# The first two triangular inverses of a delta-rule and mixture-of-experts kernel, done as 16-row triangles with TensorE corners

## The chip, the cores and the metric

The program runs on one core of a Trainium2 chip. The metric is the device time of one execution in microseconds, from the first to the last instruction and a little around it; lower is better.

## What is computed

A delta-rule attention with 4 batches, 8 heads, 768 positions and head size 48 feeds a mixture of four experts, and that feeds a gated layer:

```python
for t in range(S):
    y[:, :, t] = einsum('bhd,bhde->bhe', q[:, :, t], state)
    v_old = einsum('bhde,bhd->bhe', state, kt)
    state = state + bt * einsum('bhd,bhe->bhde', kt, vt - v_old)   # kt: normalized key
...
out += p[:, e:e + 1] * (np.maximum(x @ w1[e], 0.0) @ w2[e])         # 3072 x 384, hidden 1024, 4 experts
...
return (sigmoid(x @ w_gate) * (x @ w_val)) @ w_out                  # hidden 1536
```

## The kernel before

The 768 positions are cut into 12 steps of 64 (`C`). Within a step the recurrence is solved at once: with L the strictly triangular matrix of key products (the Gram) times the weights `w_all`, one needs the inverse of the unit triangle I + L for each of 32 (batch, head) pairs. All big products are done with operands split into a high and a low part, three matmuls for one. The attention of steps 2 to 11 is woven into the expert phases by a planner: `plan(...)` gives tasks a due time, and they are put into the stream of weight products as these pass that time. Only steps 0 and 1 come ahead of everything, in `startup()`, written out by hand in program order; the change lies in that function, in its helpers, and in the first two planned tasks.

What `startup()` does, engine by engine, each in the order of the program:

- **TensorE (PE)**: a warm-up; key Grams of steps 0 and 1 (L408, `pg`) and query products (`pq`); Grams of step 3 from `dec_a` and `dec_b` (L396); 60 padding products of zeros (`PADS`, L1297); Grams of step 2 from `KQ`, of step 4 from two `ws` tiles, of step 5 again from `dec_a` and `dec_b`; then step 0's chain: `pu` three times (inverse, corner, inverse), `py`, the transposes `pt` (L765); then the expert units `ph` (L910), with the state products `ps` (L745) of step 0 and the chain of step 1 (`pk`, `pu`) between them.
- **VectorE (DVE)**: norms, L (`LP`), masked query products (`YQ`), and then the inverse: steps 0 and 1 side by side, two 32-row triangles for each pair of a batch and a head in 128 partitions, by substitution. Substitution row s multiplies the finished columns by row s of L (`itmp`) and subtracts (`Xpp`). `invert(t0, t1)` does a piece of rows, transposes it (`x_cross`, into `ACC`) and has it copied into `XT` (`x_place`).
- **ScalarE (ACT)**: copies the Grams out of PSUM, into `LP` for steps 2 and 3 (L443), and for steps 4 and 5 (`grams_out`, L1274) into spare tiles, from which **GpSimd (POOL)** stores them in DRAM (`raw_d`) for later.
- **SP's DMA queue**: L goes out to DRAM (`ls`) and comes back in the inverse's layout (`Lpp<-ls`, by `l_read`). `both` deals the pieces of `l_out` and `l_read` out to SP's and ACT's queue by turns. `landed(t)` is a tiny DMA that waits until `t` has landed, so that what stands behind it on SP isn't issued earlier: `KQ` and the two `ws` loads (step 4's keys) stand behind the landing of `dec_b`, the next `dec_a` and `dec_b` (step 5's keys) and the first weights behind that of `KQ`.

The 32-row triangles leave the corner of the 64-row triangle out; it is put in by products with `Ld` (L's off-diagonal block) between two products with the inverse. Tiles that matter below: `XT` and `XT1`, the inverses of steps 0 and 1; `Lpp` and `Xpp`, flat scratch (`Lflat`, `Xflat`); `R`, right-hand sides; `U` in `Y`, intermediate; `rhsA`, `rhsB`, solved sides; `k2` in `Lflat`, keys for the norms of steps 2 and 3; `at`, two PSUM banks that `bank()` deals out.

Of the kernel before, what the change touches and what calls it, by code (L numbers as in the profile page):

```python
# [41 lines left out]
PADS = 60  # L42
# [74 lines left out]
def moe_delta_kernel(  # L117
# [50 lines left out]

    ident_sb = cp.tile([P, P], F32, name="ident_sb")
    mask_sb = cp.tile([P, C], F32, name="mask_sb")  # L170
# [473 lines left out]
    XC = ACC[:, 0:2].rearrange("p k c -> p (k c)").rearrange("p (t m) -> p t m", m=HC)  # L644
    Lc1 = ACC[:, 2].rearrange("p (g t) -> p g t", t=HC)
    XT1 = [gp.tile([P, 2 * STEP], F32, tag=tag, name="XT1").rearrange("p (h b t) -> p h b t", h=4, b=2) for tag in ("gv", "sg")]

    def x_cross(t0, t1):
        vec.transpose(out=XC[:, t0:t1], in_=x_view(0)[:, :, t0:t1].rearrange("p j t -> p t j"))

    def x_place(copy, c, g, t0, t1):
        i, a = divmod(g, 2)
        at, cols = slice(g * HC, (g + 1) * HC), slice(a * HC + t0, a * HC + t1)
        for k, t in enumerate(XT1 if c else [XT]):
            n = t.shape[1]
            src = XC[at, t0:t1].rearrange("p t (h c b) -> p t h c b", h=H, c=2)[:, :, k * n : (k + 1) * n, c]
            copy(out=t[at, :, :, cols], in_=src.rearrange("p t h b -> p h b t"))
# [511 lines left out]
    def startup():  # L1169
# [24 lines left out]
        l_init(0)  # L1194
        for t in (XT, Ld, *XT1, rhsA[C:112], rhsB[0:C], KI[C:112, 0], KI[0:C, 1], YQ[C:112, 0], YQ[0:C, 1]):
            nc.gpsimd.memset(t, 0.0)
# [10 lines left out]
        norm_move(0, 2)  # L1207
        q[1] = None
# [27 lines left out]
        load_ki(0)  # L1236
        spare = [((ph_p, "ph"), (acc_p, "acc1")), ((acc_p, "acc2"), (at_p, "at"))]
# [23 lines left out]
        store = [(gp, "gv"), (gp, "sg")] + [(hp, "hhi"), (hp, "hlo")] * 3  # L1261
        seats = {(4, 0): ((ph_p, "ph"), (acc_p, "acc1")), (4, 1): ((ph_p, "ph"), (acc_p, "acc2"))}
        seats |= {(5, 0): ((acc_p, "acc0"), (acc_p, "acc1")), (5, 1): ((acc_p, "acc2"), (ph_p, "ph"))}
# [13 lines left out]
        ops, cuts = [fn for _, fn in inv_ops(0, 2)], []  # L1277
        for n in range(HC - 1):
            cuts.append((cuts[-1] if cuts else 0) + 2 * min(2, n + 1))

        def invert(t0, t1, last=0):
            for fn in ops[(cuts[t0 - 2] if t0 else 0) : cuts[t1 - 2]]:
                fn()
            x_cross(t0, t1)
            for g in range(4):
                x_place(vec.tensor_copy if g < last else nc.scalar.copy, 0, g, t0, t1)
# [25 lines left out]
        invert(16, 24)  # L1312
        for hg in range(2):
            grams_mm(5, hg, KQ5)
        grams_out(5, 0)
        invert(24, 28)
        invert(28, 32, 2)
        norm_load(k2, 2)
        load_p(0)
        load_p(1)  # L1320
# [8 lines left out]
        grams_out(5, 1)  # L1329
        for g in range(4):  # L1330
            x_place(nc.gpsimd.tensor_copy, 1, g, 0, HC)
        sub = w_cast()
        for hs in sets:
            for b, pu in enumerate(quads("pu", ld, hs)):
                vec.tensor_tensor(out=R[:, b, hs], in0=R[:, b, hs], in1=pu[:, hs], op=ALU.subtract)
        pus = [quads("pu", x_of(0), hs) for hs in sets]
        for i in range(2):
            for hs, pu in zip(sets, pus):
                for rhs, at in ((rhsA, HALVES[0]), (rhsB, HALVES[1])):
                    if i and hs.start:  # L1340
                        for h in range(hs.start, hs.stop):
                            nc.scalar.activation(out=rhs[at, i, h], in_=pu[i][at, h], func=AF.Copy, scale=w_all[at, i, h : h + 1])
                        continue
                    wv = w_all[at, i, hs].unsqueeze(2).to_broadcast([C, hs.stop - hs.start, D])
                    vec.tensor_tensor(out=rhs[at, i, hs], in0=pu[i][at, hs], in1=wv, op=ALU.mult)
        q[0] = sp
        free[:] = free[:2]
        sub()
        for i in range(2):
            y_task(0, i)  # L1350
        scale_v(1)
# [34 lines left out]
        back["inv"] += first  # L1386

    with tc.manual_schedule():
        pre_lo = xp.tile([P, KT, 2 * STEP], F32R, tag="xlo", name="pre_lo")
        dec_tiles()  # L1390
        startup()
# [120 lines left out]
```

## Time and profile before

| | |
|---|---|
| median of 3 runs | 1401.55 us (1400.56 to 1403.18) |
| the profiled execution, its own time | 1401.91 us |
| span of the profiled execution | 1400.2 us |
| PE busy | 1367.8 us, 98% of the span |
| DVE, ACT, POOL busy | 1023.8, 568.9, 184.5 us |
| DMA | 237.09 MB, mean 169 GB/s |

A busy share is an average over the whole span. TensorE's granted clock is written as a share of full speed: 1.00 is 2.4 GHz and 0.50 is 1.2 GHz. The trace lists two rows for one fp32 product of the small kind (64 rows in the trace for 32 instructions in the program). A bracket at the end of a timeline's row gives the idle time of the engine just before it and what ended it.

### The profile page before, as it was taken

The numbers are of one execution on the slowest core, as the hardware profiler recorded it, in microseconds if no ns is written. First come the engines' busy times: TensorE is split into PE (matmuls) and PEld (weight loads), VectorE is DVE, ScalarE is ACT, GpSimd is POOL, SyncE is SP. The second block draws the span as 40 slices with busy tenths as digits, with TensorE's granted clock in tenths as the row PEclk, the third lists the DMA queues.
The fourth block names the chain that finished last, engine by engine and source line by source line (L and its number), as shares of the span: only waits on it lengthen the run. The fifth ranks groups of instructions, "written<-read, shape, count | busy, mean of one in ns | idle before, by whom it ended". The sixth has DMA issues, their size and how long they took to land.

```text
span 1400.2 us, 25468 instructions
## 1 busy us (share of the span) xinstructions
PE 1367.8 (98%) x10039; PEld 1131.7 (81%) x10039; DVE 1023.8 (73%) x1814; ACT 568.9 (41%) x943; POOL 184.5 (13%) x252
## 2 busy tenths in 40 slices
PE   6789999999999999999999999999999999999998
PEld 6678878878888888888888888888888888888887
DVE  6779988859998687887677887677787745444543
ACT  3665555443333343422444433344333334333333
POOL 3421222210112100011200011210000110000000
PEclk7799999999999999999999999999999999999999
DMA  9768997765556864565864465775435563434431
GB/s 244 240 208 253 322 307 226 221 176 173 160 149 157 199 174 143 145 191 137 204 185 136 152 182 143 181 194 139 132 107 133 151 177 102 132 109 121 109 107 57
DMA packets 105184, 237.09 MB, mean 169 GB/s; under 512 B 30360, under 2 KB 34648, under 8 KB 103512
## 3 DMA queue, kind: packets, MB, share of 16 engines
q1 hardware_dynamic: 86376, 189.95, 44.2%
q0 software_dynamic: 15504, 44.35, 14.0%
q8 instruction: 79, 1.29, 0.4%
q10 hardware_dynamic: 3184, 1.16, 0.4%
q14 instruction: 41, 0.34, 0.1%
HBM read 195.15 MB, written 26.79 MB: 159 GB/s over the span
## 4 chain that ended last, share of the span: by engine, by line
PE 84%; DVE 8%; DMA 4%; ACT 2%; issue 2%; ACTq 0%; SPq 0%; DVEq 0%
PE ph L910 43%; PE acc L947 35%; PE pu L630 1%; DMA raw<-in_wp 1%; DVE Xpp L144 1%; PE yt L699 1%; DVE ws L144 1%; DVE itmp L144 1%; DMA raw<-w_d 1%; PE pg L396 1%; PE ps L745 1%; DVE hlo L144 1%; PE pk L630 1%; ACT ws L231 1%; DMA Lpp<-in_wp 0%
## 5 line engine op out<-in xcount | busy, mean ns | idle before, releaser
L910 PE MATMUL ph<-xhi,ws 128*128 128x512 f32 (+1 forms) x2064 | 626.7, 387 | 1.4 <-ACT xhi L767 1.1
L947 PE MATMUL acc<-hhi,ws 128*128 128x512 f32 (+1 forms) x1632 | 493.7, 384 | 2.6 <-ACT dec_a L276 1.6
L910 PEld LDWEIGHTS ph<-xhi,ws 128*128 128x128 f32 x2064 | 381.1, 188 | 79.7 <-ACT xhi L767 1.6
L910 PE MATMUL ph<-xlo,ws 128*128 128x512 f32 (+1 forms) x1032 | 394.8, 385 | 1.5 <-DVE xlo L144 1.4
L947 PEld LDWEIGHTS acc<-hhi,ws 128*128 128x128 f32 x1632 | 302.1, 188 | 65.2 <-ACT YQ L275 2.0
L144 DVE TENSOR_TENSOR ws<-raw,ws 128x768 fp32r<-128x768 f32 x308 | 292.9, 956 | 51.4 <-ACT ws L231 47.8
L947 PE MATMUL acc<-hlo,ws 128*128 128x512 f32 (+1 forms) x816 | 312.5, 383 | 0.5 <-DVE hlo L144 0.5
L917 ACT ACTIVATE hhi<-ph 128x512 fp32r<-128x512 f32 (+1 forms) x200 | 116.1, 581 | 463.2 <-PE ph L910 463.2
L231 ACT CAST ws<-raw 128x768 fp32r<-128x768 f32 x308 | 252.6, 830 | 37.1 <-DMA raw<-w_d 21.9
L144 DVE SCALAR_TENSOR_TENSOR hlo<-ph,hhi 128x512 fp32r<-128x512 f32 (+1 forms) x200 | 133.4, 667 | 144.5 <-ACT hhi L917 144.4
L910 PEld LDWEIGHTS ph<-xlo,ws 128*128 128x128 f32 x1032 | 193.5, 188 | 42.4 <-DVE xlo L144 3.9
L947 PEld LDWEIGHTS acc<-hlo,ws 128*128 128x128 f32 x816 | 153.3, 188 | 31.0 <-DVE hlo L144 0.8
L144 DVE TENSOR_TENSOR itmp<-Xpp,Lpp 128x62 f32<-128x62 f32 (+29 forms) x344 | 158.1, 467 | 11.2 <-DMA Lpp<-ls 5.3
L144 DVE TENSOR_TENSOR Xpp<-Xpp,itmp 128x62 f32<-128x62 f32 (+29 forms) x344 | 156.7, 463 | 5.3
L926 ACT CAST hhi<-gv 128x512 fp32r<-128x512 f32 x72 | 44.7, 621 | 160.0 <-DVE gv L144 160.0
L144 DVE TENSOR_TENSOR gv<-ph,sg 128x512 f32<-128x512 f32 x72 | 49.7, 690 | 77.0 <-PE ph L910 73.7
L144 DVE TENSOR_TENSOR hlo<-gv,hhi 128x512 fp32r<-128x512 f32 x72 | 50.9, 707 | 49.4 <-ACT hhi L926 49.4
L989 POOL DMA_DIRECT2D ACC<-ctmp x39 | 34.6, 1177 | 366.4 <-DVE ctmp L144 366.4
L924 ACT ACTIVATE sg<-ph 128x512 f32<-128x512 f32 x72 | 42.8, 594 | 47.2 <-PE ph L910 47.2
L474 POOL DMA_DIRECT2D ld<-LP x12 | 8.1, 678 | 315.5 <-DVE LP L144 315.5
L144 DVE TENSOR_TENSOR ctmp<-acc,pe 128x512 f32<-128x512 f32 (+1 forms) x57 | 35.4, 656 | 8.6 <-PE acc L947 7.8
L630 PEld LDWEIGHTS pu<-R,XT 64*64 64x64 f32 x1024 | 18.3, 140 | 12.6 <-issue 9.3
(189 smaller groups left out, 837.6 us busy)
## 6 DMA issues: line engine op xcount, KB each, us to landing
raw<-in_wp SPq DMA_DIRECT2D x200, 384.0 KB, 3.2
raw<-w_d SPq DMA_DIRECT2D x108, 384.0 KB, 3.8
ACC<-ctmp POOLq DMA_DIRECT2D x33, 256.0 KB, 5.4
KQ<-in_kg SPq DMA_DIRECT2D x7, 896.0 KB, 7.9
Lpp<-ld POOLq DMA_DIRECT2D x8, 768.0 KB, 11.0
pe<-p_d SPq DMA_DIRECT2D x23, 256.0 KB, 5.9
dec_a<-in_wp SPq DMA_DIRECT2D x15, 384.0 KB, 5.7
Lpp<-in_wp SPq DMA_DIRECT2D x14, 384.0 KB, 5.6
```

What stands on the lines that cost most here:

```text
L144: return fn(*args, **kw)
L231: nc.scalar.copy(out=w[:, 0], in_=t)
L396: nc.tensor.matmul(out=pg[i][b * C : (b + 1) * C, j], lhsT=src[b][ROWS[i], 0, h], rhs=src[b][ROWS[i], :, h], start=True, stop=True,)
L630: nc.tensor.matmul(out=ps[r][HALVES[k], h], lhsT=lhsT, rhs=rhs, start=True, stop=True)
L699: nc.tensor.matmul(out=yt[o : o + m, k, b], lhsT=f[:, h * D : h * D + m], rhs=rt, start=True, stop=True)
L745: nc.tensor.matmul(out=ps[C:112, h], lhsT=KI[0:112, 0, i, h], rhs=rhsA[:, i, h], start=True, stop=True)
L910: nc.tensor.matmul(out=res[q], lhsT=lt, rhs=rt, start=(k == 0 and j == 0), stop=(k == KT - 1 and j == 2))
L917: nc.scalar.activation(out=hh, in_=res[0], func=AF.Relu)
L924: nc.scalar.activation(out=sg, in_=res[0], func=AF.Sigmoid)
L926: nc.scalar.copy(out=hh, in_=gv)
L947: nc.tensor.matmul(out=acc_t[d][:, :w], lhsT=lt, rhs=rt, start=(u == 0 and j == 0), stop=(u == nf - 1 and j == 2),)
L989: nc.gpsimd.dma_start(out=a, in_=t, accum_op=ALU.add)
```

## The change

The inverse of steps 0 and 1 works on 16-row triangles: four in place of two for each pair, two of them side by side in the free dimension (`X16`, `inv16`), so that there are 15 substitution rows in place of 31, each in one multiplication and one subtraction. `x_cross` transposes the result in two halves, and `place` writes it to its spot in `XT` for all 128 partitions at once, times a 0/1 column `own` that says which partitions own it. The corner of each 32-row triangle is then computed on TensorE: `corner1` multiplies the far half of the inverse by a masked Gram (`GM`, made at the start from 128 more key products and 8 masked copies), `corner1_out` scales the result by `w_v`, `corner2` multiplies by the near inverses (`XSm`), and `corner2_out` subtracts the result into `XT`. For step 0 this happens in `startup()`, for step 1 it goes behind the two `ps` tasks.

Other moves: all four reads of L are issued by SP, ahead of the load of `dec_a`; `PADS` is 12; of the Grams of steps 4 and 5 only the first quarter stays ahead of step 0's chain, and the other three quarters, with their copies and stores, come behind `pt`; step 2's Grams are copied out during the `pu` products; the key load for `k2` comes behind step 1's first corner product, and the loads of `pe` a little later.

```diff
-PADS = 60
+PADS = 12
...
+    def inv16(s0, s1):
+        for s in range(s0, s1):
+            nj, nt = s + 1, QC - 1 - s
...
+            row = Lflat[:, o : o + 2 * QC * (HC + 1)].rearrange("p (k f) -> p k f", k=2)[:, :, :nt]
+            col, tgt = X16[:, :, :nj, s : s + 1], X16[:, :, :nj, s + 1 :]
...
+            vec.tensor_tensor(
+                out=tmp, in0=col.to_broadcast(sh), in1=row.unsqueeze(2).to_broadcast(sh), op=ALU.mult
+            )
+            vec.tensor_tensor(out=tgt, in0=tgt, in1=tmp, op=ALU.subtract)
...
+    def by_act(out, in_, m):
+        nc.scalar.activation(out=out, in_=in_, func=AF.Copy, scale=own[:, m : m + 1])
...
+    def corner_mm(c, ps, lhs, rhs):
+        for h in range(H):
+            for b in range(2):
+                for i in range(2):
+                    nc.tensor.matmul(
+                        out=ps[HALVES[i], 2 * h + b], lhsT=lhs(h, b)[HALVES[i]], rhs=rhs(h, b)[HALVES[i]],
+                        start=True, stop=True,
+                    )
+
+    def corner1(c, ps, G):
+        far = lambda h, b: x_at(c, h, b).rearrange("p (a k t) -> p a k t", a=2, k=2)[:, :, 1]
+        corner_mm(c, ps, lambda h, b: G[h // 4][:, h % 4, b], far)
...
         KQ3 = [t[:112, : 2 * H * C].rearrange("p (a h t) -> p a h t", a=2, h=H) for t in dec_mem[2:4]]
+        q[0] = sp
+        l_read(0)
         sp.dma_start(out=KQ3[0], in_=kg_view(3)[0])
-        l_read(0)
-        q[0] = sp
...
-        grams(2, KQi)
-        invert(0, 16)
+        inv16(0, QC // 2)
+        x_cross(0, QC // 2)
+        for m in (1, 3, 0, 2):
+            place(by_act, [XT], XC, 0, m, 0, QC // 2)
         for hg in range(2):
-            grams_mm(4, hg, KQ4)
-            grams_out(4, hg)
+            grams_mm(2, hg, KQi)
+        grams_mm(4, 0, KQ4)
+        inv16(QC // 2, QC - 1)
+        x_cross(QC // 2, QC)
+        place(by_act, [XT], XC, 0, 1, QC // 2, QC)
+        place(by_dve, [XT], XC, 0, 3, QC // 2, QC)
+        nc.gpsimd.memset(XSm[0], 0.0)
+        vec.transpose(out=XS, in_=X16.rearrange("p k j t -> p j k t"))
+        ps = at_p.tile([P, 2 * H, HC], F32, tag="at", name="pc")
+        corner1(0, ps, GM[0])
+        for m in (0, 2):
+            place(by_act, XSm, XS, 0, m)
+        corner1_out(0, ps)
+        ps = at_p.tile([P, 2 * H, HC], F32, tag="at", name="pc")
+        corner2(0, ps)
...
+        corner2_out(0, ps)
...
         for i in range(2):
             tr_task(0, i)
+        grams_mm(4, 1, KQ4)
+        for hg in range(2):
+            grams_mm(5, hg, KQ5)
+        for at in ((4, 1), (5, 0), (5, 1)):
+            grams_out(*at)
...
+        def corner(n):
+            s_task(0, n)
+            ps = bank([P, 2 * H, HC], "pc")
+            (corner2 if n else corner1)(1, ps, *(() if n else (GM1,)))
+            (corner2_out if n else corner1_out)(1, ps)
+            if n == 0:
+                norm_load(dec_mem[4], 2)
+
         for i in range(2):
-            plan(0.0, lambda i=i: s_task(0, i), "pe")
+            plan(0.0, lambda i=i: corner(i), "pe")
```

How this moves instructions is seen best in three places. On PE, from the padding to the first products of step 0's chain (`pg` are Grams, `pc` corner products, `pu` the chain), before:

```order
L1297 MATMUL acc_134<-pre_lo 64x48 x60
L396 MATMUL pg<-KQ 64x128 x32
L396 MATMUL pg<-ws 64x128 x32
L396 MATMUL pg<-dec_a 64x128
L396 MATMUL pg<-dec_b 64x128 x2
...
L630 MATMUL pu<-R,XT 64x48 x32
L630 MATMUL pu<-Y_113,Ld 64x48 x32
```

and now:

```order
L1378 MATMUL acc_136<-pre_lo 64x48 x12
L399 MATMUL pg<-KQ 64x128 x32
L399 MATMUL pg<-ws 64x128 x16
L695 MATMUL pc<-XT,Lpp 64x32 x32
L695 MATMUL pc<-Y_116,Lpp 64x32 x32
L633 MATMUL pu<-R,XT 64x48 x32
L633 MATMUL pu<-Y_115,Ld 64x48 x32
```

Both corner products stand behind the Grams of step 2 and the first half of step 4's, ahead of the first `pu`. On the SP queue, around the reading of L, before:

```order
L1167 DMA ls<-LP_119 32x16x32 x2
L1221 DMA dec_a<-in_kg 112x1024
L1167 DMA Lpp<-ls 32x1024 x2
L1235 DMA dec_b<-in_kg 112x1024
L344 DMA KI<-in_kt 64x768
L345 DMA KI<-in_kt 64x768
L1233 DMA landed_d<-dec_b 1x1
L337 DMA KQ<-in_kg 112x2048
L1292 DMA ws<-in_kg 112x1024 x2
```

and now:

```order
L1229 DMA ls<-LP_121 32x16x32 x2
L523 DMA Lpp<-ls 32x1024 x4
L1294 DMA dec_a<-in_kg 112x1024
L1306 DMA dec_b<-in_kg 112x1024
L347 DMA KI<-in_kt 64x768
L348 DMA KI<-in_kt 64x768
L1304 DMA landed_d<-dec_b 1x1
L340 DMA KQ<-in_kg 112x2048
L1373 DMA ws<-in_kg 112x1024 x2
```

Four reads of L now stand ahead of `dec_a`, where two stood behind it. On ACT, from the copies of `py` to the first copy of a state product, before:

```order
L714 COPY Y_113<-py 128x384 x2
L767 CAST xhi<-pt 128x3x128 x2
L231 CAST ws<-raw 128x768 x2
L917 ACTIVATE hhi<-ph 128x256
L748 COPY rhsA<-ps 48x384
```

and now:

```order
L776 COPY Y_115<-py 128x384 x2
L829 CAST xhi<-pt 128x3x128 x2
L1366 COPY tmp<-pg 128x4x2x64 x2
L1366 COPY Xpp<-pg 128x4x2x64 x2
L1366 COPY ACC<-pg 128x4x2x64 x2
L234 CAST ws<-raw 128x768 x2
L979 ACTIVATE hhi<-ph 128x256
L810 COPY rhsA<-ps 48x384
```

Six copies of Grams stand between the cast of step 0's result and the casts of the second and third pair of weights (`ws`).

## Rows read from the trace of the kernel before

**Rows 1.** Windows: stretch, length, busy per engine, granted clock, DMA share, GB/s

```profile
0.00:60.00 60.00, 40.79 (x911) 36.53 (x912) 44.39 (x175) 30.68 (x75) 23.23 (x38) 0.72 0.83 242
60.00:100.00 40.00, 35.10 (x616) 31.52 (x616) 30.40 (x57) 20.47 (x40) 14.13 (x20) 1.00 0.76 227
```

**Rows 2.** Timeline, PE: start, us, line, op, tiles, shapes, count, idle

```profile
24.05 0.48 PE L396 MATMUL pg<-dec_b 48*64 48x128 f32 x2 [1.98 <-DMA dec_b<-in_kg]
...
34.17 1.20 PE L396 MATMUL pg<-KQ 48*64 48x128 f32 x35 [1.67 <-issue]
...
35.22 3.27 PE L396 MATMUL pg<-ws 48*64 48x128 f32 x60
...
49.10 1.97 PE L630 MATMUL pu<-R,XT 64*64 64x48 f32 x64 [5.14 <-ACT XT L657]
...
57.09 1.22 PE L765 MATMUL pt<-ident_sb,Y 128*128 128x128 f32 x6
58.88 0.51 PE L910 MATMUL ph<-xhi,ws 128*128 128x256 f32 x2 [0.57 <-ACT xhi L767]
```

**Rows 3.** Timeline, DVE, columns as in group 2

```profile
14.61 5.59 DVE L144 TENSOR_TENSOR YQ<-pq,mask_sb 64x512 f32<-64x512 f32 x8
25.54 0.19 DVE L144 TENSOR_TENSOR itmp<-Xpp,Lpp 128x31 f32<-128x31 f32 x1 [5.34 <-DMA Lpp<-ls]
...
34.50 0.48 DVE L144 TENSOR_TENSOR itmp<-Xpp,Lpp 128x136 f32<-128x136 f32 x2
...
42.68 0.61 DVE L144 STREAM_TRANSPOSE ACC<-Xpp 128x256 f32<-128x256 f32 x1
...
59.71 2.63 DVE L144 TENSOR_TENSOR ws<-raw,ws 128x768 fp32r<-128x768 f32 x2 [0.30 <-DMA raw<-in_wp]
...
62.60 0.54 DVE L144 COPY rhsB<-ps 48x384 f32<-48x384 f32 x1
```

**Rows 4.** Timeline, SP queue (times are those of issuing)

```profile
15.83 0.33 SPq L1221 DMA_DIRECT2D dec_a<-in_kg  x1
17.60 0.78 SPq L1167 DMA_DIRECT2D Lpp<-ls  x2
...
24.02 0.27 SPq L1233 DMA_DIRECT2D landed_d<-dec_b  x1
...
24.76 0.95 SPq L1292 DMA_DIRECT2D ws<-in_kg  x2
30.07 0.23 SPq L1233 DMA_DIRECT2D landed_d<-KQ  x1
```

**Rows 5.** Timeline, ACT engine and its DMA queue

```profile
19.50 0.80 ACTq L1167 DMA_DIRECT2D Lpp<-ls  x2
...
27.77 1.07 ACT L443 COPY LP<-pg 128x512 f32<-128x512 f32 x2 [0.47 <-PE pg L396]
```

**Rows 6.** One tile, `ws`, to 60 us: time from issue to landing

```profile
DMA to landing us min/median/max: 6.6/7.8/9.0
```

**Rows 7.** Windows as in group 1, for the granted clock

```profile
28.00:30.00 2.00, 2.00 (x63) 2.00 (x62) 2.00 (x14) 0.85 (x2) 0.00 (x0) 0.82 1.00 281
...
32.00:34.00 2.00, 0.50 (x15) 0.25 (x7) 2.00 (x12) 0.00 (x0) 0.00 (x0) 1.00 1.00 307
...
36.00:38.00 2.00, 2.00 (x44) 2.00 (x40) 2.00 (x10) 1.98 (x5) 0.00 (x0) 0.50 0.77 228
...
52.00:54.00 2.00, 2.00 (x95) 1.88 (x88) 1.72 (x6) 1.24 (x2) 1.79 (x4) 0.85 0.30 102
```

**Rows 8.** Timeline, PE, from 62 us, columns as in group 2

```profile
64.74 0.31 PE L630 MATMUL pk<-rhsA,KS 48*64 48x48 f32 x2
...
70.98 1.15 PE L630 MATMUL pu<-Y,Ld 64*64 64x48 f32 x64
```

**Rows 9.** DMA issues to 75 us: count, KB each, median us to landing

```profile
raw_d<-hhi POOLq DMA_DIRECT2D x3, 256.0 KB, 6.1
...
Lpp<-in_kt SPq DMA_DIRECT2D x1, 768.0 KB, 9.5
```

More of the change, by code (lines that the diff above doesn't have):

```diff
@@ L167, in moe_delta_kernel @@
     dr1 = pool("dram1", 1, space=DRAM)
+    QC = HC // 2
     ident_sb = cp.tile([P, P], F32, name="ident_sb")
+    own = cp.tile([P, 8], F32, name="own")
+    w_v = cp.tile([P, 2, 2, H], F32, name="w_v")
     mask_sb = cp.tile([P, C], F32, name="mask_sb")
@@ L642, in ks_task @@
             vec.tensor_tensor(out=R[:, b], in0=V[:, b], in1=pk, op=ALU.subtract)
-    XC = ACC[:, 0:2].rearrange("p k c -> p (k c)").rearrange("p (t m) -> p t m", m=HC)
+    XC, XS = (ACC[:, k].rearrange("p (t m) -> p t m", m=HC) for k in range(2))
     Lc1 = ACC[:, 2].rearrange("p (g t) -> p g t", t=HC)
     XT1 = [gp.tile([P, 2 * STEP], F32, tag=tag, name="XT1").rearrange("p (h b t) -> p h b t", h=4, b=2) for tag in ("gv", "sg")]
-    def x_cross(t0, t1):
-        vec.transpose(out=XC[:, t0:t1], in_=x_view(0)[:, :, t0:t1].rearrange("p j t -> p t j"))
@@ new lines, in x_cross, with by_dve, by_pool @@
+    def x_cross(t0, t1):
+        vec.transpose(out=XC[:, t0:t1], in_=X16.rearrange("p k j t -> p t (k j)")[:, t0:t1])
+    def by_act(out, in_, m):
+        nc.scalar.activation(out=out, in_=in_, func=AF.Copy, scale=own[:, m : m + 1])
+    def by_dve(out, in_, m):
+        vec.tensor_scalar(out=out, in0=in_, scalar1=own[:, m : m + 1], scalar2=None, op0=ALU.mult)
+    def by_pool(out, in_, m):
+        nc.gpsimd.tensor_scalar(out=out, in0=in_, scalar1=own[:, m : m + 1], scalar2=None, op0=ALU.mult)
@@ new lines, in place @@
+    def place(by, dst, src, c, m, t0=0, t1=QC):
+        for k, t in enumerate(dst):
+            n = t.shape[1]
+            part = src[:, t0:t1].rearrange("p t (h c b) -> p t h c b", h=H, c=2)[:, :, k * n : (k + 1) * n, c]
+            by(t[:, :, :, m * QC + t0 : m * QC + t1], part.rearrange("p t h b -> p h b t"), m)
+    XSm = [Lflat[:, : 2 * H * C].rearrange("p (h b t) -> p h b t", h=H, b=2)]
+    T16 = Y[1].rearrange("p i f -> p (i f)")[:, : H * C].rearrange("p (h b a t) -> p h b a t", h=H, b=2, a=2)
@@ L1207, in startup @@
         norm_move(0, 2)
+        for i in range(2):
+            for b in range(2):
+                pool_q.dma_start(
+                    out=w_v[HALVES[i], :, b],
+                    in_=w_all[HALVES[b], 0:4].rearrange("p (c i) h -> p c i h", i=2)[:, :, i],
+                )
         q[1] = None
@@ L1236, in startup @@
         load_ki(0)
+        vec.tensor_reduce(
+            out=own, in_=ident_sb.rearrange("p (g x) -> p g x", x=QC), op=ALU.add, axis=mybir.AxisListType.X
+        )
+        vec.tensor_tensor(out=own[:, 0:4], in0=own[:, 0:4], in1=own[:, 4:8], op=ALU.add)
+        for c, t in ((0, KQi), (1, KQ1)):
+            for b in range(2):
+                pg = bank([P, H, C], "pg")
+                for h in range(H):
+                    for i in range(2):
+                        nc.tensor.matmul(
+                            out=pg[HALVES[i], h], lhsT=t[b][ROWS[i], 0, h], rhs=t[b][ROWS[i], 0, h], start=True, stop=True
+                        )
+                near = lambda a: a.rearrange("p h (a k t) -> p h a k t", a=2, k=2)[:, :, :, 0]
+                own_ = own[:, 1:4:2].unsqueeze(1).unsqueeze(3).to_broadcast([P, 4, 2, QC])
+                for k, g in enumerate(GM[c]):
+                    vec.tensor_tensor(out=near(g[:, :, b]), in0=near(pg[:, 4 * k : 4 * k + 4]), in1=own_, op=ALU.mult)
         spare = [((ph_p, "ph"), (acc_p, "acc1")), ((acc_p, "acc2"), (at_p, "at"))]
@@ L1328, in startup @@
             vec.tensor_copy(out=U[:, 1, hs], in_=pu[1][:, hs])
[L1329 to L1332, printed above, removed]
+        for hg in range(2):
+            raw_out(2, hg)
         for hs in sets:
@@ L1360, in startup @@
             tr_task(0, i)
+        grams_mm(4, 1, KQ4)
+        for hg in range(2):
+            grams_mm(5, hg, KQ5)
+        for at in ((4, 1), (5, 0), (5, 1)):
+            grams_out(*at)
         q[0] = pool_q
```

80 lines of the change are left out of this document (47 added, 33 removed).

## The prediction

> **What bounds the kernel now.** I read the windows first. From 60 us on PE is busy 35.1 of 40 us, and the page gives it 98% of the whole span; in the first 60 us it is busy 40.8, at a mean granted clock of 0.72 [rows 1]. The weight stream behind the start follows PE, so a start that is shorter by so much ends the program earlier by nearly as much, and the start is the only part that the change touches. Next the timelines. DVE waits 5.34 us for L, begins the inverse at 25.54 [rows 3], and PE's first chain product comes at 49.10, after 5.14 us of waiting for the last copies into `XT` [rows 2]. From the first substitution row to the chain: 23.6 us. From there PE reaches the end of `pt` at 58.31 (57.09 + 1.22) [rows 2], and step 1's first product `pk` at 64.74 [rows 8]. These three points, 49.10, 58.31 and 64.74, carry the sum. What stands in front of PE in the order also matters: `dec_b`, awaited until 24.05 [rows 2], and the loads issued only after its landing [rows 4].
>
> **The inverse itself.** Before DVE can start, it now has its 5.59 us of `YQ` [rows 3] and eight masked copies of 128 elements, each below one `YQ` operation (0.70), about 0.28, so 2.2 us; PE makes 128 more trace rows of Grams (some 4 us at the 31 ns of the row at 49.10 [rows 2]) ahead of `YQ`'s products, which delays these by about 1.5 us. DVE is free at 14.61 + 5.59 + 2.2 + 1.5, about 24. L was last issued at 19.50 by ACT, behind `dec_a` of 15.83 [rows 4, 5], and landed at 25.54; without that load ahead I expect 22.5 to 25.5. So the inverse starts at 24 to 25.5; I take 24.5. It has 30 dependent operations, 91 elements on average. One of 31 elements is 0.19 busy, a pair of 136 takes 0.48 [rows 3]; 0.28 each gives 8.4 us, and two transposes of 0.61 [rows 3] make 9.7. With one copy by ACT of 0.5 (half of the pair at 27.77 [rows 5]) the near half stands in `XT` at about 34.7. The copies of step 3's Grams on ACT end near 30 and do not hold this up.
>
> The Trainium skill (Trainium Kernel Development and Optimization, Key Constraints) says that DMAs of all issuing engines run on the same 16 engines, and that issuing from several saves issue time alone. By it one queue for L costs two issues, 0.8 us by the trace; that lies within the start of 24 to 25.5 and changes nothing in the sum.
>
> **What PE has to do first.** Here the gain is cut. `dec_a` now stands behind four reads of L, the last three of which wait for the pieces that ACT wrote (ACT's own reads waited until 19.50 [rows 5]). It is issued at about 20 instead of 15.83, and `dec_b` lands not at 24.02 but at about 25.3 (25.0 to 27.0). All behind that landing moves with it, by 1.3: `KQ` from 30.07 [rows 4] to 31.4, and the slower of the two `ws` loads, issued about 25.2 [rows 4] and 9.0 us on the way [rows 6], from 34.2 to 35.5. Both corner products stand behind the Grams of step 2 and half of step 4's. Step 2's 64 rows take 2.2 to 3.5 us (34 ns in the row at 34.17, 55 ns in that at 35.22 [rows 2]) and end by 34.9, before `ws` is there. Step 4's 32 rows then take 1.1 to 1.75: PE reaches the corner at 36.9, some 2.2 us after `XT` is ready. So DMA, not DVE, sets the corner's start.
>
> **The corner.** Each product has 64 trace rows. The chain products of 64 rows took 1.97 us at 49.10 (clock 0.50) [rows 2] and 1.15 at 70.98 (clock 1.00) [rows 8]; these are the two ends. A masked DVE pass of about 0.70 and two hand-overs of 0.15 follow each, so a round is 2.15 to 3.0. The clock came up in the window from 28 after PE's work that began at 24.05, fell again by the window from 36 after the pause in that from 32 (0.50 busy), and came up in that from 52 after `pu` began at 49.10 [rows 2, 7]. After the change PE works from 31.4 with a pause of about half a microsecond, so I take the upper level for both rounds: 4.3 us, `pu` at 41.2, that is 7.9 us earlier; at the lower level 6.0, and 6.2 us earlier. For the chain I take the old 9.2 us to the end of `pt`, with its start at the lower level again; step 2's four copies on ACT replace step 5's and lie beside PE's work. End of `pt`: 50.4.
>
> **Behind `pt`.** Three quarters of the Grams of steps 4 and 5, which lay under the inverse, now stand on PE's path: 96 rows at 34 ns, 3.3 us. Step 1's two corner products add 2 times 1.15. That is 5.6. The waits of before, 0.57 [rows 2] and about as much for the low part, go: minus 1.1. A new wait comes: ACT copies the last pair of Grams (1.07 [rows 5]) before it casts weights, so the first cast is done some 5.3 us after `pt`; DVE then takes 3.2 us for two subtractions, a low part and the copy of the first state product (59.71 to 63.14 [rows 3]), and only at 8.5 is a PSUM bank free for the second state product, which PE could start at 7.6. Plus 0.8. Together 5.3 us more between `pt` and `pk` (4.2 if no wait is new, 6.2 if the products are slow).
>
> **The sum.** -7.9 + 5.3 = -2.6 us on the profiled execution: 1401.9 to 1399.3. Against the median of 1401.55, which lies 0.4 below: 1399.0. What a measurement of this kernel can tell from no change is about 0.2%, 2.8 us; the forecast stands at that bound.
>
> **The rivals.**
> *A, the clock stays low.* If the pauses between the small products keep the clock at 0.50, as it stood in the window from 36 although PE was busy throughout [rows 7], the rounds take 6.0: -6.2 + 5.3 = -0.9, 1400.7. The Trainium skill (TensorE: Matmul & The Clock Gate, Part 1) gives small products a floor of about 25 ns from start to start even at the upper level; no row here bears that out, since 1.15 us for 64 rows is 18 ns [rows 8]. By it the four corner products would cost 1.8 us more, with 1400.8.
> *B, the clock stays up through the chain.* Then the three `pu` products, up to 1.97 us each [rows 2], would shrink towards 1.15 each [rows 8], at most 2.5 in all; hand-overs between them leave about 1.5: -4.1, 1397.5. For it speaks that PE is more steadily busy from 31 on; against it the fall after the short pause at 32 [rows 7]. The same page's section says that the lower level is the default and activity ends it; the trace agrees at 28 and 52.
> *C, transfers take it back, slower than before.* Six stores of 256 KB and the 768 KB of norm keys [rows 9], 2.36 MB, move behind `pt`. At 227 GB/s [rows 1] that is 10.4 us; DMA's free 24% [rows 1] of the 20 us that follow is 4.8. The rest, 5.6 us, would be late weights: -2.6 + 5.6 = +3.0, 1404.6. It decides where the weight loads of the fourth and fifth pair, issued behind these, land after PE wants them. Against it: their casts also come 5 us later relative to `pt`.
> *D, it does not do what it says.* The substitution becomes no shorter per row: 30 operations at 0.41 and an inverse that starts at 25.5 put `XT` at 39.5, 2.6 us behind PE: no gain, 1401.5.
>
> **How the numbers follow.** Forecast 48%, of which 27 lie beyond the bound on the fast side and 21 within it; A 18%, within; B 18%, faster; C 12%, slower; D 4%, within. Faster 45%, within 0.2% 43%, slower 12%. The range goes from 1395.2 (B, and half of what the shorter 4.2 us behind `pt` and the earlier `dec_b` would add) to 1403.2 (C at three quarters of its price); some 2 in 10 lie outside, most of it in C.
>
> **What would show it.** DVE's first substitution at 24 to 25.5 and the last transpose some 10 us later; `dec_b` at 25.3 and step 4's first Gram awaiting `ws` near 35.5; the first corner product at 36.9 with `XT` long ready; `pu` near 41.2; `pt` ending near 50.4; then 96 Gram rows in 3.3 us, a wait ahead of the second state product, and `pk` some 11.7 us after `pt`. The forecast is wrong if corner products start straight after `XT` (then DVE is the bound and the gain larger), if their 64 rows take 2 us, or if PE waits for weights between 60 and 80 us.

## The result and the profile after

The changed kernel takes 1415.20 us (median of 5 runs, 1409.34 to 1416.75) against 1400.88 for the kernel before in the same comparison: ratio 1.009, 95% interval 1.0076 to 1.0105. That is 12.6 us slower by the ratio and 14.3 by the medians; forecast were 1399.0 and at most 1403.2. The profiled execution is the slowest of the five (1416.75); it has a span of 1415.0 us, the kernel before's 1400.2, so 14.8 us are to be found in these two traces, some 2 more than the runs differ by. Medians in microseconds below stand against a kernel before of 1400.8 to 1402.0 in each comparison; where parts are added up, a ratio is multiplied by 1401.

SP's queue in the changed kernel (issue time, duration, line, transfer; answers to [rows 4]):

```profile
13.77 2.56 SPq L1229 DMA_DIRECT2D ls<-LP  x4
18.57 4.96 SPq L523 DMA_DIRECT2D Lpp<-ls  x4
23.57 0.42 SPq L1294 DMA_DIRECT2D dec_a<-in_kg  x1
...
30.18 0.28 SPq L1304 DMA_DIRECT2D landed_d<-dec_b  x1
...
36.48 0.23 SPq L1304 DMA_DIRECT2D landed_d<-KQ  x1
```

The four reads of L hold SP for 4.96 us, `dec_a` goes out at 23.57 instead of 15.83, and `dec_b` has landed at 30.18 instead of 24.02. DVE, as to [rows 3]:

```profile
25.87 0.19 DVE L144 TENSOR_TENSOR itmp<-Xpp,Lpp 128x30 f32<-128x30 f32 x1
...
34.90 0.61 DVE L144 STREAM_TRANSPOSE ACC<-Xpp 128x256 f32<-128x256 f32 x1
...
46.62 0.69 DVE L144 TENSOR_TENSOR Y<-pc,w_v 128x512 f32<-128x512 f32 x1 [10.12 <-PE pc L695]
```

The inverse is as short as forecast: it begins at 25.87, without a wait for L, and its last transpose for `XT` ends at 35.51 (34.90 + 0.61). Then DVE waits 10.12 us for PE. PE (as to [rows 2, 8]; `pc` is a corner product):

```profile
36.55 3.69 PE L399 MATMUL pg<-KQ 48*64 48x128 f32 x64 [1.41 <-DMA KQ<-in_kg]
...
41.29 1.76 PE L399 MATMUL pg<-ws 48*64 48x128 f32 x27 [0.67 <-DMA ws<-in_kg]
42.64 0.36 PE L695 MATMUL pc<-XT,Lpp 64*64 64x32 f32 x2
...
47.57 3.63 PE L695 MATMUL pc<-Y,Lpp 64*64 64x32 f32 x64 [0.98 <-DVE Y L144]
52.13 1.16 PE L633 MATMUL pu<-R,XT 64*64 64x48 f32 x33 [0.93 <-DVE XT L144]
...
66.08 2.06 PE L695 MATMUL pc<-XT,Lpp 64*64 64x32 f32 x64
...
77.22 1.02 PE L633 MATMUL pu<-R,XT 64*64 64x48 f32 x53 [1.03 <-issue]
...
83.96 0.58 PE L1009 MATMUL acc<-hhi,ws 128*128 128x256 f32 x1 [3.07 <-issue]
...
124.85 0.73 PE L1009 MATMUL acc<-hhi,ws 128*128 128x512 f32 x2 [2.90 <-DVE ws L144]
```

The loss, point by point against the kernel before: `pu` 3.0 us late (52.13 against 49.10), the end of `pt` 2.9 (61.24 against 58.31), `pk` 8.7 (73.42 against 64.74), the second state's `py` 12.3 (92.07 against 79.75), and 14.8 after the wait for weights at 124.85, which in the kernel before is 0.39. Later waits are of 1.6 us at most in both. What happens between `pk` and `py` is in the windows (stretch, length, PE, PEld, DVE, ACT, POOL busy, granted clock, DMA share, GB/s):

```profile
72.00:80.00 8.00, 6.97 (x201) 6.29 (x200) 2.30 (x6) 2.11 (x5) 0.00 (x0) 1.00 1.03 349
80.00:84.00 4.00, 0.93 (x42) 0.68 (x34) 4.00 (x7) 2.25 (x3) 0.00 (x0) 0.84 0.66 203
84.00:88.00 4.00, 4.00 (x21) 3.78 (x25) 0.70 (x1) 0.00 (x1) 0.00 (x0) 0.50 0.70 198
```

The DMA engines are full from 72 to 80, PE waits 3.07 us for nothing that the trace names, and the clock falls to 0.50 behind it, the lower of its two levels (1.2 GHz), so that the next products take nearly twice as long (a group of three of `acc` 0.64 us from start to start behind the wait, 0.35 at 74.50).

### The profile page after: what moved, and what is told of

It is laid out like the page before. It is cut to its first block, busy times and chain, and to the rows that moved or that the text cites. A ratio compares the mean times of both kernels' runs of the same rounds, so it can differ in the third digit from the quotient of the medians.

```text
span 1415.0 us, 25989 instructions
## 1 busy us (share of the span) xinstructions
PE 1384.4 (98%) x10327; PEld 1147.9 (81%) x10327; DVE 1013.5 (72%) x1735; ACT 567.4 (40%) x938; POOL 186.9 (13%) x260
## 3 DMA queue, kind: packets, MB, share of 16 engines
q0 software_dynamic: 15632, 44.36, 14.8%
## 4 chain that ended last, share of the span: by engine, by line
PE 84%; DVE 7%; DMA 5%; issue 2%; ACT 1%; SPq 1%; ACTq 0%; DVEq 0%
PE ph L972 43%; PE acc L1009 34%; PE pu L633 1%; DVE ws L144 1%; DMA raw<-in_wp 1%; PE yt L761 1%; PE pg L399 1%; DMA Y<-YT 1%; DVE hlo L144 1%; PE ps L807 1%; PE pc L695 1%; DVE Xpp L144 1%; DMA ws<-in_kg 1%; PE pk L633 1%; DVE YQ L144 1%
## 5 line engine op out<-in xcount | busy, mean ns | idle before, releaser
L234 ACT CAST ws<-raw 128x768 fp32r<-128x768 f32 x308 | 253.4, 832 | 44.4 <-DMA raw<-in_wp 26.2
L144 DVE TENSOR_TENSOR itmp<-Xpp,Lpp 128x120 f32<-128x120 f32 (+46 forms) x298 | 148.4, 498 | 6.3
L144 DVE TENSOR_TENSOR Xpp<-Xpp,itmp 128x120 f32<-128x120 f32 (+46 forms) x298 | 147.5, 495 | 5.8
```

The costliest lines, as they stand in the source:

```text
L144: return fn(*args, **kw)
L234: nc.scalar.copy(out=w[:, 0], in_=t)
```

## Experiments

**The parts undone one at a time in the changed kernel.** First L by two queues again, with `dec_a` ahead of it:

```diff
-        q[0] = sp
-        l_read(0)
         sp.dma_start(out=KQ3[0], in_=kg_view(3)[0])
+        l_read(0)
+        q[0] = sp
```

> The changed kernel with one part undone: L of steps 0 and 1 is read back by two queues again, and the first half of step 3's operand (dec_a) is issued on SP ahead of it. Theory 1 (in the changed kernel the four L transfers hold SP from 18.6 to 23.5 us, so dec_b lands at 30.2 instead of 24.0, KQ at 36.5 instead of 30.1, and the Grams of steps 2 and 4, which stand ahead of the corner products on TensorE, end at 42.6): dec_b lands at 24 to 26, KQ at 30 to 32, the first corner product begins at 36.5 to 38 (the far half of XT is placed at 37.05), pu at 46.5 to 48 instead of 52.1, time 4 to 6 us below the changed kernel: 1409 to 1411. Rival 2 (the loss lies behind pt, in the full DMA queues of 72 to 80 us, and takes up what comes early): pu at 46.5 to 48 as well, but the time within 2 us of the changed kernel, 1413 to 1416.

Measured: 1413.40 us, ratio 1.008 (1.0061 to 1.0099). `pu` came at 47.51 and `pt` ended at 56.44, as theory 1 had it; the time fell by 1.8 only, as rival 2 forecast, but not where it put the loss. The wait at the first `acc` product grew from 3.07 to 4.16 us, and PE was still 5.0 us ahead of the changed kernel behind it (78.92 against 83.96) and 6.7 behind the late weights (118.14 against 124.85). At the end 1.6 are left between the two profiles. The largest loss lies far behind the start:

```profile
78.92 0.37 PE L1009 MATMUL acc<-hhi,ws 128*128 128x256 f32 x1 [4.16 <-issue]
...
482.12 0.21 PE L807 MATMUL ps<-rhsA,KI 112*48 112x48 f32 x1 [1.93 <-issue]
```

PE waits 1.93 us for nothing that the trace names, and the clock falls behind it (0.79 from 482 to 490). The changed kernel has no such wait there. Whether it comes from the earlier start is not shown.

The corner ahead of the Grams on PE (`grams_mm(2, 0)` between the two corner products, `grams_mm(2, 1)` and `grams_mm(4, 0)` behind them):

> The changed kernel with the first corner product ahead of the Grams of steps 2 and 4 on TensorE, a half of step 2's Grams between the two corner products and the rest behind the second. Theory 1 (the corner products wait for Grams that wait for transfers): the first corner product begins at 36.5 to 38 instead of 42.6, at the low clock still 3.7 us long, the second at about 42.5, the rest of the Grams 3.1 us, pu at 48.5 to 50 instead of 52.1, time 2 to 4 us lower: 1411 to 1413. Rival (the operands of the corner, XT and XS through ScalarE, are what is late): the first corner product begins no earlier than 40, and the time is within 1 us of the changed kernel.

Measured: 1414.75. The first corner product began at 38.10 and `pu` at 49.94, as expected, but `pt` ended at 61.16 against 61.24: between them now lie a wait of 0.57 us for ACT's copies of step 4's Grams and one of 0.89 without a cause. The end came no sooner. The small products that keep PE busy (`PADS = 60`):

> The changed kernel with the 60 small products of the kernel before behind step 3's Grams, in place of 12. Theory 3 (the low clock, 0.5 in 30 to 50 us, makes the two corner products 3.6 us each, 2.0 at the full clock): 48 more products of 25 to 60 ns fill 1.2 to 2.9 of the 3.2 us in which TensorE waits for KQ; if they bring the clock up, KQ's Grams take 2 instead of 3.7 us, the corner products 2.0 each, pu is at 46 to 48 instead of 52.1 and the time 4 to 6 us lower, 1409 to 1411. Rival: the clock stays at 0.5 until the chain itself is dense, nothing moves, 1414 to 1416.

Measured: 1419.41. The clock of 36 to 44 us rose from 0.50 to 0.79 and `pu` came at 50.44; `KQ` had also landed 1.9 us sooner in this profile (34.60), so that not all of it is the clock's. Yet the median rose by 4. Why it rose was not found.

The two corner products of step 1 left out (`corner(n)` keeps only `s_task(0, n)` and the load of the norms):

> The changed kernel without the two corner products of step 1 (it leaves out that part of step 1's inverse, so that step 1's result is not the reference's). Theory 7 (behind pt TensorE has no idle time, so that work put there costs its whole length, and the 128 product records take part in the waits for instructions as well): 2 x 2.06 us of products go, pk begins at 69 instead of 73.4, and with the full-queue waits 3 to 5 us shorter too: 6 to 9 us below the changed kernel, 1406 to 1409. Rival (only the products count): 4 to 4.5 us, 1410.5 to 1411.5. Rival (later waits for weights take it back): under 3 us.

Measured: 1409.21, ratio 1.0053 (1.0035 to 1.0072): 6.0 us less by the medians and 5.2 by the ratios, for 4.1 us of products. The wait at the first `acc` product is still there (2.26).

The stores of the late Grams issued behind the norms instead of at once:

```diff
-            grams_out(*at)
+            grams_out(*at, late=True)
...
         first += [(7.5, "", move2)]
+        first += [(7.6, "", fn) for fn in sends]
```

> The changed kernel with its six stores of Grams behind pt (1.5 MB) issued some 28 us later, at about 92 us, where the DMA share is 0.06; copies and products stay. Theory 6 (the DMA engines are full from 72 to 80 us, share 1.01 to 1.04, and TensorE's waits without a cause, 1.03 us at 76.2 and 3.07 at 80.9, last as long as they do because of that; the second one costs the clock too, 0.5 until 88): the share of 72 to 80 falls to 0.8 or less, the two waits to 1.5 us or less together, the clock stays at 1.0, the second state product's py begins 4 to 6 us sooner than 92.1, time 3 to 6 us below the changed kernel, 1409 to 1412. Rival (the waits are there whatever the DMA engines do, as the kernel before's 1.15 at 68.1 with a share of 0.93): the waits stay over 3 us together and the time within 1.5 us of the changed kernel.

Measured: 1419.01. The waits fell to 0.58 and 1.68, `py` came at 88.37 instead of 92.07 as expected, but the stores then met the stores of L and the weights: the stretch from 92 to 104 has a DMA share of 0.94, the clock falls at 104, and PE waits 3.25 us for weights until 124.2. The theory is right about the place and wrong about the sum. With two queues the same:

> The changed kernel with L by two queues as in the first run and the six stores at about 90 us. In the first run pt ended 4.8 us sooner than in the changed kernel and the time fell by 1.8 only: a wait without a cause of 4.16 us at 74.8 and 1.9 at 480, and 1.5 for weights at 116. Theory 6 (the full DMA queues take back what comes early): the waits of 70 to 90 fall under 2 us together, the clock stays up, the time 6 to 9 us below the changed kernel, 1406 to 1409. Rival (the waits do not hang on the stores): 1412 to 1414 as without the move.

Measured: 1415.51. No gain either; moving the bytes is no cure.

**Parts alone in the kernel before.** One queue for L:

> The kernel before with one part of the change alone: L of steps 0 and 1 comes back by SP alone, and ahead of the first half of step 3's operand (dec_a) instead of behind it. Theory 1 (on SP the four transfers wait for the stores of L to land, and what is queued behind them is late by 6 us): dec_a, dec_b and KQ land 5 to 6 us later than at 22, 24 and 30, the fifth step's operand at 43 instead of 37.5; the 32-row inverse on VectorE (25.5 to 47) still ends last ahead of pu, so pu moves by 0 to 1 us and the time by 0 to 2: 1401 to 1403.5. Rival (the late Grams stand ahead of the placing of XT on ScalarE and delay pu as well): pu 3 to 5 us later, 1404 to 1407.

Measured: 1403.02, ratio 1.0011 (1.0001 to 1.002). `dec_b` landed at 27.89 and KQ at 34.08, 4 us late; `pu` moved by 0.9. The Grams behind `pt`:

> The kernel before with one part of the change alone: the Grams of step 4's second half and of step 5 (96 rows), their six copies and six stores stand behind pt, at the place and with the buffers of the changed kernel; the 32-row inverse, the two queues for L and the 60 small products stay. Theory 4 (moved behind pt they cost their rows and also fill the DMA queues, so that TensorE waits for nothing that the trace shows for 4.1 us in 76 to 84, loses its clock until 89 and gets weights late at 122): pu unchanged at 49.1, pk 3 to 4 us later, waits without a cause longer than before's 2.8, time 6 to 11 us above the kernel before, 1407 to 1412. Rival 5 (only the rows count, the full queues come from the load of the norms at 69 us, which this kernel issues at its old place): 2.5 to 3.5 us above, 1403.5 to 1404.5.

Measured: 1404.35, ratio 1.002 (1.001 to 1.0029), 2.8 us, as rival 5 had it for the rows alone. `pu` was not unchanged: in the profile L landed later (the inverse began at 26.44) and `pu` came at 50.75, so 1.7 of the 2.6 us by which the span grew lie ahead of the moved rows. Theory 4 failed: the 1.5 MB of stores made no weights late. The DMA engines were full here too (share 1.00 from 68 to 72 us, 0.97 from 72 to 80), with a wait of 1.92 us and the clock at 1.00.

**The cause that no line of the diff shows.** The time from issue to landing (the last number, a median) of the 64 KB stores of L by SP split the runs so far in two groups, with the change and without, whatever else was changed. From the lists of DMA issues, first the kernel before, then the changed one:

```profile
ls<-LP SPq DMA_DIRECT2D x8, 64.0 KB, 2.7
...
ld<-LP SPq DMA_DIRECT2D x4, 64.0 KB, 2.1
```

```profile
ls<-LP SPq DMA_DIRECT2D x8, 64.0 KB, 4.1
...
ld<-LP SPq DMA_DIRECT2D x4, 64.0 KB, 3.8
```

The diff adds two small tiles behind `ident_sb`, `own` (32 bytes a partition) and `w_v` (128). All tiles behind them move up by 160 bytes in SBUF: from 128 bytes past a multiple of 256 to 32 past one. The rows that these stores carry are of 128 bytes (ACT's queue, which from 10 to 19 us carries little else than four of them, moves 0.26 MB in 2112 packets). Padding `own` brings the old place back:

```diff
-    own = cp.tile([P, 8], F32, name="own")
+    own = cp.tile([P, 96], F32, name="own")[:, :8]
```

> The changed kernel with one number changed: the new tile own is 384 bytes of each partition long instead of 32 (8 floats of it are used), so that the two new tiles push all later tiles of SBUF up by 512 bytes instead of 160, and these start where they did modulo 256. Theory 8 (the shift by 160 bytes makes transfers of short rows dearer: the 64 KB stores of L, rows of 128 bytes, land 3.5 to 4.1 us after their issue by SP in every kernel with the change and 2.1 to 2.8 in every one without, whatever else they differ in, and the POOL queue's packets take 14.7 to 15.0% of the span instead of 14.0): the stores of L fall back to 2.1 to 2.8 us, the POOL queue to 14.0 to 14.3%, dec_b lands 1 to 2 us sooner, the DMA waits of 70 to 125 us shrink, time 2 to 6 us below the changed kernel: 1409 to 1413. Rival (place in SBUF has nothing to do with it, the stores are slow because they meet other traffic): stores as in the changed kernel, time within 1.5 us of it.

Measured: 1410.29, ratio 1.0059 (1.004 to 1.0078), 4.9 us less for a tile's length. SP's queue in this kernel:

```profile
17.89 2.29 SPq L523 DMA_DIRECT2D Lpp<-ls  x4
20.22 0.42 SPq L1294 DMA_DIRECT2D dec_a<-in_kg  x1
...
27.32 0.28 SPq L1304 DMA_DIRECT2D landed_d<-dec_b  x1
```

The four reads take 2.29 us instead of 4.96, `dec_b` has landed 2.9 us sooner, `pu` comes at 48.15. These are single profiles, and such times scatter: in the other four with the shifted tiles and one queue for L (`corner_first`, `pads_60`, `no_second_corner`, `stores_late`) the reads took 2.54 to 5.18 us and `dec_b` landed at 28.65 to 31.16; with the tiles at the old place it landed at 27.32 here and at 27.89 in `one_queue_before`. The expectation on the stores came true in part:

```profile
ls<-LP SPq DMA_DIRECT2D x8, 64.0 KB, 3.1
...
ld<-LP SPq DMA_DIRECT2D x4, 64.0 KB, 3.8
```

The first group fell from 4.1 to 3.1 us, the second did not move, where 2.1 to 2.8 was expected of both; so the second does not hang on the place alone. The late weights of 2.90 us are gone, but the wait at the first `acc` product is not, nor are the full DMA engines ahead of it (share 1.02 from 66 to 76 us):

```profile
79.59 0.58 PE L1009 MATMUL acc<-hhi,ws 128*128 128x256 f32 x1 [3.05 <-issue]
```

The other direction, an unused tile in the kernel before and nothing else:

```diff
+    gap = cp.tile([P, 40], F32, name="gap")
     mask_sb = cp.tile([P, C], F32, name="mask_sb")
```

> The kernel before with an unused tile of 160 bytes a partition behind ident_sb and nothing else, so that all its tiles lie where they lie in the changed kernel modulo 256. Theory 8: the 64 KB stores of L land 3.5 to 4.1 us after their issue by SP instead of 2.1 to 2.7, the POOL queue takes 14.6 to 15.0% of the span instead of 14.0, and the time rises by 2 to 5 us, 1403 to 1406. Rival: nothing moves, 1400 to 1402.

Measured: 1405.68, ratio 1.003 (1.0019 to 1.0041). DVE waits longer for L:

```profile
28.22 0.19 DVE L144 TENSOR_TENSOR itmp<-Xpp,Lpp 128x31 f32<-128x31 f32 x1 [7.29 <-DMA Lpp<-ls]
```

The inverse begins 2.7 us later than at 25.54, and `pu` comes 2.7 later (51.80). The engines' own work did not get longer (DVE busy 1024.6 us against 1023.8, ACT 569.0 against 568.9), so it is the transfers that pay. That the place of the tiles costs this time is shown from both sides. The page's rows of POOL's queue (packets, MB, share of the 16 engines) carry it over the whole span; the kernel before, the changed one, `aligned` and `before_shifted`:

```profile
q0 software_dynamic: 15504, 44.35, 14.0%
```

```profile
q0 software_dynamic: 15632, 44.36, 14.8%
```

```profile
q0 software_dynamic: 15632, 44.36, 13.9%
```

```profile
q0 software_dynamic: 15504, 44.35, 14.8%
```

Two more places, with a `gap` of 32 floats (multiples of 256) and of 48 (64 past one):

> The kernel before with an unused tile of 128 bytes in the same place: the tiles, which start 128 bytes past a multiple of 256 in the kernel before, now start at multiples of 256. If whole multiples count, transfers of rows of 256 bytes and more get shorter (the POOL queue under 14.0% of the span) and the time falls by 0 to 3 us, 1398 to 1401.5; if only the rows of 128 bytes matter and these never straddle at either place, nothing moves.

> The kernel before with an unused tile of 192 bytes, so that all later tiles start 64 bytes past a multiple of 256. Which property of the place counts: if it is that rows of 128 bytes straddle a multiple of 256 (as at 32), the POOL queue takes 14.6 to 15.0% of the span, the stores of L 3.5 us and more, and the time is 1403.5 to 1406 as in before_shifted. If it is a place that is no multiple of 64, it is as before: 13.9 to 14.1%, 2.1 to 2.7 us, 1400 to 1402.

```profile
q0 software_dynamic: 15504, 44.35, 13.0%
```

```profile
q0 software_dynamic: 15504, 44.35, 14.6%
```

Measured: 1400.62 with POOL's queue at 13.0% (ratio 0.9995, 0.9985 to 1.0006, no change), and 1405.20 with 14.6% (1.0024, 1.0014 to 1.0033). So a start at a multiple of 64 is not enough. What fits is whether a row of 128 bytes straddles a multiple of 256: at 0 and 128 none does, at 32 and 64 half of them do. A start that is no multiple of 128 would fit as well; no run tells these two apart. (SP's stores landed after 3.2 us there, a little under the 3.5 expected.) That the share is lower still at 0 than at 128 would fit longer rows, which straddle at 128; that was not tried by itself. The Trainium skill (DMA: Bandwidth & Descriptors, How a descriptor splits into AXI transactions) says that a descriptor is cut into transactions at multiples of 256 bytes, and that one which starts off them pays for the bytes before its start. The lowest share at 0 agrees; that 64 past was no dearer than 32 past (14.6 against 14.8%) does not follow from the bytes before the start.

**Do the parts add up?** Padding and two queues together, the same at multiples of 256 (`own` of 64 floats), and the first without step 1's corner:

> The same padding together with L by two queues. Theory 8 and theory 1 together: stores of L at 2.1 to 2.8 us, dec_b at 24 to 25, pu at 46 to 47.5, and the gain of the earlier chain kept because the transfers behind it are quicker: 5 to 9 us below the changed kernel, 1406 to 1410. Rival: as two_queues without the padding, 1413.4.

> The changed kernel with L by two queues and the tile own at 256 bytes, so that all later tiles start at multiples of 256. In the kernel before this place took the POOL queue from 14.0 to 13.0% of the span and moved the time by nothing that can be told. Against aligned_two_queues (1408.7): the POOL queue at 13.0%, the time the same or up to 2 us lower, 1406.5 to 1409.

> The changed kernel with the padded tile, L by two queues and without step 1's two corner products (it leaves that part of step 1's inverse out, so its result is not the reference's). If the parts add up (place in SBUF 4.9, second corner 6.0, Grams behind pt 2.8, one queue 1.5), this kernel, which has only the Grams left of these, stands 6 us below aligned_two_queues and 2.8 less the gain of the shorter chain above the kernel before: 1401.5 to 1403.5; with the chain's gain of 1.6 (pu at 47.5 instead of 49.1) about 1402.8. Rival (the second corner was dear only because transfers were slow): only its 4.1 us of products come off, 1404 to 1405. Rival (the shorter chain is worth nothing): 1404 to 1405 as well, with pk at 64 to 64.5 in both.

Measured: 1408.74 (ratio 1.0048, 1.003 to 1.0066), 1407.52 (1.004, 1.0024 to 1.0056) and 1404.03 (1.0009, 0.9998 to 1.0019). By ratios: the place in SBUF costs 4.2 alone (4.3 and 4.5 undone), the second corner 5.2 and 5.5, the Grams behind `pt` 2.8, the single queue 1.5 (1.4 and 1.5 undone). That is 13.8 of 12.6 measured; what is left over is -1.2. The last kernel, with only the Grams of these four, stands 1.3 above the kernel before, and 2.8 - 1.3 gives 1.5. Both are remainders, of the shorter inverse with step 0's corner, `PADS` and the moved loads, none of which was undone alone. They are smaller than the intervals that they come from: 1.3 us each way for the Grams, 1.5 for the last kernel. And its median of 1404.03 lies where the expectation put a shorter chain that is worth nothing (1404 to 1405). So a gain of the shorter inverse is not shown.

**The price of a corner product.** Its 64 rows took 3.63 us at the lower clock and 2.06 at the upper, the chain's 1.97 and 1.15 [rows 2, 8]. The chain's go through the four quadrants of the array in turn and into two PSUM banks, the corner's through the two on the diagonal and into one:

```diff
-                        out=ps[HALVES[i], 2 * h + b], lhsT=lhs(h, b)[HALVES[i]], rhs=rhs(h, b)[HALVES[i]],
+                        out=ps[i][HALVES[i ^ b], 2 * h + b], lhsT=lhs(h, b)[HALVES[i]], rhs=rhs(h, b)[HALVES[i]],
...
-            ps = bank([P, 2 * H, HC], "pc")
+            ps = [bank([P, 2 * H, HC], "pc") for _ in range(2)]
```

> aligned_two_queues with the corner products of every second block written to the other half of the PSUM partitions, one bank for each half of the contraction, so that successive products go through all four quadrants of the array in turn as the chain's do, instead of the two on the diagonal. The passes on VectorE behind them are cut in four, about 0.4 us more for each round and some 1 us for step 1's second. (The corner blocks of every second head half end in the wrong half, so the result is not the reference's; shapes and number of products are the same.) The step of the prediction that took a corner product's price from the chain's products (64 rows in 1.97 us at the lower clock, 1.15 at the upper) measured 3.63 and 2.06. Theory 9 (two quadrants in turn hide half of what four hide): the 64 rows take 1.1 to 1.4 us at the upper clock and 2.0 to 2.4 at the lower, pk comes 2.5 to 4.5 us sooner, time 2 to 4.5 us below aligned_two_queues: 1404 to 1407. Rival (32 columns instead of 48 or the shape 64 x 32 are what is slow): rows as before, 3.6 and 2.06 us, time 1408 to 1411 with the extra passes.

Measured, in PE's timeline:

```profile
38.09 1.99 PE L695 MATMUL pc<-XT,Lpp 64*64 64x32 f32 x61
...
62.92 1.13 PE L695 MATMUL pc<-XT,Lpp 64*64 64x32 f32 x62 [2.43 <-DVE rhsB L144]
...
68.62 1.13 PE L695 MATMUL pc<-Y,Lpp 64*64 64x32 f32 x62 [0.83 <-DVE rhsB L144]
```

So the shape 64 x 64 x 32 is not what is slow: the same products take 1.99 and 1.13 us here, the chain's price. What makes the difference is how they are laid out; the run changes the order of the quadrants and the number of PSUM banks together, and which of the two it is, is not shown. The time did not follow (1409.17, ratio 1.0057, 1.0039 to 1.0075), as the rival had it: each corner product now takes both of the two banks, PE waits 2.43 and 0.83 us behind `pt` for DVE's copies out of them, and `pk` comes at 72.0 instead of 68.2.

A nearer row than the chain's stood in the trace of the kernel before. Its padding products go through the same two quadrants into one bank, with 48 columns, and from 29 to 31 us PE does nothing else:

```profile
29.00:31.00 2.00, 2.00 (x76) 2.00 (x74) 2.00 (x13) 0.00 (x0) 0.00 (x0) 1.00 1.00 293
```

That is 26 ns a row at the upper clock, against the chain's 18 and the corner's 32.

## Why the prediction was wrong

- **What bounds the kernel now**: right for work behind `pt`: PE is full from there on, and 4.1 us of products cost 5.2. That a shorter start ends the program earlier by nearly as much held with the place put right (`aligned_two_queues` against `aligned`: `pu` 1.45 us sooner, the span 1.3 shorter), but not in `two_queues` (4.8 and 1.8).
- **The inverse itself**: right in length, 9.6 us against 9.7. It began at 25.87, 0.4 later than the latest forecast: not L held it up but DVE, which began `YQ` at 20.24, 5.6 us later than before, where 3.7 had been put for the masked copies and the Grams ahead of them.
- **What PE has to do first**: the failed step. `dec_b` was put at 25.3 (25.0 to 27.0) and landed at 30.18; KQ at 36.48 instead of 31.4, the corner at 42.64 instead of 36.9. I took the four reads of L at their old durations and did not ask where the new tiles lie. Between the profiles of `after` and `aligned` 2.9 of the 4.9 us come from the place in SBUF, the rest from the order on SP (with the scatter of such landings, 28.65 to 31.16 against 27.32 and 27.89, the place's part is 0.8 to 3.8). In the kernel before, one queue alone cost `dec_b` 3.9 us, not the two issues of 0.8. A transfer's duration was carried over from a row, although the change moved its address.
- **The corner**: the second failed step, and the one that alone takes the gain away. A round was 2.15 to 3.0; they took 4.93 and 4.56. The price came from products that run through four quadrants into two banks, and the clock stayed at the lower level (0.50 from 36 to 52 us) as rival A had it, its 6.0 for both rounds being too short too. In `aligned_two_queues` the step before came out as forecast (`dec_b` at 25.12, `KQ` at 31.23, the corner at 37.33), and `pu` still came at 46.70 instead of 41.2. Corner start 5.7 late and rounds 5.2 longer are the 10.9 us between a `pu` at 41.2 and at 52.13.
- **The chain**: right, 9.1 us against 9.2.
- **Behind `pt`**: right in sum, 5.75 us against 5.3 (96 rows in 2.9, the two corner products 2.06 each instead of 1.15, the wait for a bank did not come since the longer corner products covered it).
- **Rival C**, late weights, came with 2.5 us at 124.85, later than thought. The moved bytes, its cause as forecast, do not suffice: `aligned` moves all of them without a late weight there, and `before_64` moves none and waits 2.16 us for weights at 112.33.
- **Not in the sum at all**: the wait of 3.07 us at the first `acc` product and the clock that it costs, 3.6 us between `pk` and `py`. Its place hangs on the count of PE's instructions: in nine of the eleven variants of the changed kernel it stands at that product or the next, `no_second_corner` with 128 product records fewer among them, and in `pads_60`, which has 48 products or 96 records more, it stands 95 records earlier. In the changed kernel 127 records lie between it and the wait at 76.19, in the kernel before as many between the waits at 68.09 and 74.90. The trace shows what arrives. The page of the changed kernel, and the DMA queues from 81.5 to 81.6 us:

```profile
q8 instruction: 81, 1.33, 0.4%
```

```profile
q8 instruction: 1, 0.02, 69.5%
```

This queue moves 16 KB packets of instructions, 81 for 10327 product records, 79 for 10039 in the kernel before, 80 and 82 with 128 records fewer and 96 more: about 127 records each. Of the packets around the wait (80.90 to 83.96) one begins at 81.55, inside the wait, and ends at 82.66; PE goes on 1.3 us later. In the ten variants that have a wait of this kind there it ends 1.2 to 1.7 us behind such a packet. So PE waits for its next block of instructions. Why the block comes late is argued only: full DMA engines fit (1.68 us with the stores moved, 3.07 without, and 2.23 against 4.16 with two queues), but no run changed the fetch alone.
- **The account**: 10.9 at `pu`, -0.1 in the chain, 0.5 behind `pt`, 3.6 up to `py` and 2.5 of late weights are the 17.4 us between -2.6 and +14.8 of the profiles. Two figures of the prediction do not come out of their own parts: without a new wait the time behind `pt` is 4.5 more, not 4.2, and half of what that and an earlier `dec_b` could add to B's 1397.5 ends near 1396.3, not at 1395.2. Neither bears on the result.

## What to carry to other kernels

Before a duration is carried over from a trace, ask whether the change moves the buffer: a small tile added in front shifts every later one, and a shift by 160 bytes, which leaves rows of 128 bytes across multiples of 256, cost this kernel 4 us. Price a small product by one that uses the same quadrants in the same order and as many PSUM banks. Work moved out of an idle stretch into a full one cost its whole length here and, for the second corner, more. No complete variant here beat the kernel before: the best form of the change is `aligned_256` at 1407.52, and the kernel before at multiples of 256 (1400.62) is no faster than it was.

## What was unexpected of the hardware

- The start of the tiles modulo 256 moved POOL's queue between 13.0, 14.0, 14.6 and 14.8% of the span for the same 44.4 MB (0, 128, 64 and 32 bytes past).
- Products of 64 x 64 x 32 through two diagonal quadrants took 57 ns a record at the lower clock and 32 at the upper (3.63 and 2.06 us for 64); through four, into two banks instead of one, 33 and 18 (1.99 for 61, 1.13 for 62).
- An earlier chain is not an earlier end: with two queues `pt` ended 4.8 us sooner and the program 1.8; most of the rest went at 480 us.
- PE's instructions come in packets of 16 KB, some 127 product records each, and PE waits where one is late (3.07 us in the changed kernel).
